# A transformer block's opening in halves: scale weights by column halves, first queries by halves, six heads projected ahead of the shift

## The chip, the cores and the metric

The kernel runs on one core of a Trainium2 chip. Its engines work side by side, each through its own list of instructions in order: TensorE (PE in the profile: matmuls; PEld: the loading of their stationary operand), VectorE (DVE), ScalarE (ACT), GpSimd (POOL) and SyncE (SP), which here issues most of the loads. The metric is the time of one execution on the device in microseconds (us), as the median of the runs; less is better.

## The reference, cut to what matters

One block: a normalisation with scale and shift out of a condition vector, attention over the last keys of a cache, then a gated feed-forward stage.

```python
mod = (_silu(c) @ w_mod).reshape(c.shape[0], 6, 1, -1)
sa, ca, ga, sb, cb, gb = (mod[:, 0], mod[:, 1], ...)
h = _layernorm(x) * (1 + ca) + sa                # x: 2048 tokens x 1024
x = x + ga * _A_ref(h, A_k_cache, A_v_cache, A_wq, A_wo)
h = _layernorm(x) * (1 + cb) + sb
x = x + gb * _B_ref(h, B_w_gate, B_w_up, B_w_down)
# _A_ref: q = h @ wq (32 heads of 128); scores over the last 512 keys (4 key groups);
#         softmax; values; then @ wo.    _B_ref: silu(h @ w_gate) * (h @ w_up) @ w_down
```

All tensors are bf16. `c` is one row of 1024 numbers, `w_mod` 1024 x 6144: its first 1024 columns give the shift `sa`, the next 1024 the scale `ca`, then the gate `ga`.

## The kernel before

Tokens go through in four chunks of 512, each of four tiles of 128. For a chunk, 32 heads are worked one after another in the loop of L1037: queries ahead of time, scores (`scores`, four matmuls of 512 columns into the banks `SCB` 2 to 5), the exponential on ACT (`exps`, two of 1024 numbers a row), the product with the values (`pv`, 16 matmuls of 129 columns), and a reciprocal and a multiplication on DVE. Then comes the output projection, and after the last chunk the feed-forward stage. Queries are projected four heads before they are used (`LEAD`); the first eight heads (`PLAIN`) plainly with 8 matmuls, the others in pairs by seven products that need sums of weights and of inputs (`weight_sums`, `input_sums`, on DVE).

The order of the work is written out by hand. Each `T.op` puts an instruction on one engine's list, with waits on the semaphores of whatever wrote or read its buffers. Nothing reorders it later. DMAs are issued by SP in program order.

The change touches the stretch before the first scores, the opening, and the first heads of the loop. Before the change it goes so:

- SP issues: 4 tiles of x, the scale columns of `w_mod` in 8 row blocks of 256 KB (`load_wm(0)`), the query weights of heads 0 to 3 (`load_wq(0)`, two halves of 512 KB by rows), the keys, the shift columns in 8 row blocks (`load_wm(1)`), the query weights of heads 4 to 7 (`load_wq(1)`), and the values in four parts.
- ACT, DVE and PE turn the condition into 8 columns `sc` (L344 to L350).
- DVE computes mean and variance of tiles 0 and 1 by `ln_stats` and `ln_rstd`; ACT sums up tiles 2 and 3 (`sums_1`), DVE scales these sums (`sums_2`); POOL takes the power -0.5. `ln_norm` writes the normalised tiles.
- PE multiplies the scale columns with `sc` (`mod_open(0, kc)`: 8 matmuls of one column for each row block), with a filler matmul (`keep_warm`) here and there, and turns the tiles (`open_turn`, 8 transposes each), which DVE or ACT evicts into `h_sb[1]`, 128 x 8 x 512. When all eight row blocks are in, DVE forms the gain `g1`, and DVE and ACT multiply the turned input by it, 512 tokens at a time (L514 to L519).
- From L1002: PE projects heads 0, 1 and 2 out of this unshifted input, with the shift columns (`mod_open(1, kc)`) between; DVE copies the shift `sa`; PE turns the keys (`turn_keys`), multiplies the query weights of heads 0 to 3 with `sa`, 32 matmuls of one column, and projects head 3. ACT adds these four columns to the four heads (L1021), and DVE writes the shifted input `h_sb[0]` (L1024), which all later heads read.
- In the loop, iterations 0 to 3 project heads 4 to 7 (`qproj`, 8 matmuls and a copy on DVE). Also in chunk 0, from iteration 0 on, one step of the next chunk's normalisation (`ln1[1]`) is taken in each iteration, and from iteration 3 on steps of the gate's computation (`mod_ga`) (L1074). A step is a load, half of a tile's statistics, a normalisation, or two scaled rows (`ln_scale`, L376).

## Time and profile before

| what | value |
|---|---|
| median of 3 runs | 1174.58 us (1174.24 to 1174.76) |
| the profiled execution | 1188.51 us |
| its span, first to last instruction | 1186.7 us |
| granted TensorE clock in it | 0.995 |
| PE busy in the span | 1150.3 us (97%) |
| DVE busy | 814.2 us (69%) |
| ACT busy | 502.1 us (42%) |
| first one-column matmul of the scale | 7.62 us |
| first query matmul | 16.29 us |
| first exponential | 28.56 us |

Times within the profile count from the span's start. A line of the timeline gives start, length, engine, source line, operation, output and input, the count, and in brackets how long the engine had been idle and what ended that. Matmuls and transposes stand under the lines of the helpers that issue them, L265 and L269, so they are told apart by their shapes: 128x1 is a column of scale or shift, 128x512 a query or score matmul, 128x129 a value product. Some matmul records are missing.

### The profile page before, as it was taken

How to read it: one execution, taken by the hardware profiler on the slowest of the kernel's cores; microseconds unless marked ns; L12 is line 12 of the kernel's file. 1: busy time of each engine (PE TensorE's matmuls, PEld its weight loads, DVE VectorE, ACT ScalarE, POOL GpSimd, SP SyncE). 2: the span in 40 equal slices, each digit the busy share in tenths (PEclk: the TensorE clock that was granted, in tenths of full speed). 3: DMA queues.
4: the chain of work that ended last, by engine and by line, in shares of the span. 5: the costliest groups of instructions: out<-in, count | busy, mean ns of one | idle time of the engine just before them, and what ended most of it. 6: DMA issues, size and time to landing. Idle time of an engine off the chain costs nothing.

```text
span 1186.7 us, 20667 instructions
## 1 busy us (share of the span) xinstructions
PE 1150.3 (97%) x7721; PEld 665.4 (56%) x7838; DVE 814.2 (69%) x1800; ACT 502.1 (42%) x750; POOL 20.6 (2%) x41
## 2 busy tenths in 40 slices
PE   6999999999999999999999999999989999999998
PEld 4677646777557776478764444444433444444443
DVE  4888647987638887358857688887335977776214
ACT  4777503666216664056741344444110344444110
POOL 1000000000000000000000000000000000000000
PEclk9999999999999999999999999999989999999999
DMA  9999796999859987769949666566896332321633
GB/s 302 230 262 233 212 364 215 288 251 224 285 188 281 266 204 226 280 181 273 262 104 367 204 183 207 178 188 175 288 176 140 106 106 73 97 82 63 247 134 133
DMA packets 282852, 245.56 MB, mean 207 GB/s; under 512 B 109952, under 2 KB 245120, under 8 KB 282752
## 3 DMA queue, kind: packets, MB, share of 16 engines
q1 hardware_dynamic: 252304, 179.74, 58.2%
q10 hardware_dynamic: 30448, 64.50, 16.0%
q8 instruction: 62, 1.02, 0.4%
q14 instruction: 38, 0.31, 0.1%
HBM read 189.27 MB, written 30.41 MB: 185 GB/s over the span
## 4 chain that ended last, share of the span: by engine, by line
PE 85%; DMA 6%; DVE 4%; issue 2%; SPq 1%; ACT 1%; POOL 0%; POOLq 0%; DVEq 0%
PE ps L265 85%; DMA arena<-arena 3%; DMA arena<-x_mid 1%; DVE arena L580 1%; DMA arena<-in_w_mod_dram 1%; DMA arena<-wq_sums 1%; SPq L284 1%; DVE arena L376 0%; DVE arena L717 0%; DVE arena L412 0%; DVE arena L646 0%; DVE arena L421 0%; DVE arena L919 0%; DVE arena L847 0%; ACT arena L967 0%
## 5 line engine op out<-in xcount | busy, mean ns | idle before, releaser
L265 PE MATMUL ps<-arena 128*128 128x129 bf16 (+5 forms) x7672 | 1146.5, 309 | 28.4 <-DVE arena L469 3.9
L265 PEld LDWEIGHTS ps<-arena 128*128 128x128 bf16 (+1 forms) x7789 | 661.8, 98 | 512.3 <-issue 22.3
L700 ACT ACTIVATE arena<-ps 128x1024 bf16<-128x1024 f32 x256 | 251.3, 1022 | 39.3 <-PE ps L265 36.3
L580 DVE TENSOR_TENSOR arena<-arena 128x512 f16<-128x512 bf16 (+3 forms) x510 | 222.8, 479 | 26.0 <-DMA wo_sums<-arena 11.0
L640 ACT ACTIVATE arena<-ps 128x256 f32<-128x256 f32 x134 | 51.4, 384 | 167.2 <-PE ps L265 166.8
L1211 DVE TENSOR_TENSOR arena<-ps,arena 128x512 f16<-128x512 f32 x112 | 77.1, 688 | 36.9 <-PE ps L265 36.6
L1204 ACT ACTIVATE arena<-ps 128x512 f32<-128x512 f32 x112 | 66.9, 597 | 73.5 <-PE ps L265 73.5
L717 DVE TENSOR_TENSOR arena<-ps,arena 128x512 bf16<-128x512 f32 x128 | 88.5, 691 | 4.5
L1233 ACT ACTIVATE ps<-ps 128x512 f32<-128x512 f32 x56 | 32.6, 582 | 130.3 <-PE ps L265 130.3
L919 DVE TENSOR_TENSOR arena<-ps,arena 128x512 f32<-128x512 f32 x34 | 23.4, 688 | 87.1 <-PE ps L265 87.0
L646 DVE TENSOR_TENSOR arena<-ps,arena 128x256 bf16<-128x256 f32 x180 | 75.5, 419 | 10.9 <-PE ps L265 6.9
L1223 DVE TENSOR_TENSOR arena<-ps,arena 128x512 bf16<-128x512 f32 x56 | 38.5, 687 | 27.3 <-ACT arena L1218 27.3
L716 DVE RECIPROCAL arena<-ps 128x4 f32<-128x4 f32 x128 | 23.0, 180 | 38.1 <-PE ps L265 37.5
L1218 ACT ACTIVATE arena<-ps 128x512 f16<-128x512 f32 x56 | 33.3, 594 | 31.6 <-PE ps L265 31.6
L922 DVE TENSOR_TENSOR arena<-ps,arena 128x512 bf16<-128x512 f32 x22 | 15.1, 688 | 45.3 <-PE ps L265 45.3
L412 DVE BATCH_NORM_STATS2 arena<-arena 128x6 f32<-128x512 bf16 x56 | 38.3, 686 | 6.3 <-DMA arena<-x_mid 6.1
L950 DVE SCALAR_TENSOR_TENSOR arena<-arena 128x512 f32<-128x512 bf16 x56 | 41.6, 742 | 0.1
L1218 ACT ACTIVATE arena<-arena 128x512 f16<-128x512 f16 x56 | 34.9, 622 | 7.7 <-DVE arena L1211 7.7
L847 DVE TENSOR_TENSOR arena<-arena 128x1024 f16<-128x1024 bf16 (+1 forms) x48 | 29.7, 684 | 5.7 <-DMA arena<-arena 5.7
L363 POOL TENSOR_TENSOR arena<-arena 128x1 f32<-128x1 f32 x30 | 18.1, 602 | 877.9 <-DVE arena L361 874.8
L421 DVE TENSOR_SCALAR arena<-arena 128x1024 bf16<-128x1024 bf16 x28 | 15.1, 540 | 25.9 <-DMA arena<-arena 23.9
L871 ACT ACTIVATE arena<-ps 128x512 f32<-128x512 f32 x12 | 6.8, 596 | 59.2 <-PE ps L265 51.3
(62 smaller groups left out, 230.4 us busy)
## 6 DMA issues: line engine op xcount, KB each, us to landing
arena<-wo_sums ACTq DMA_DIRECT2D x46, 512.0 KB, 9.2
arena<-in_A_wq_dram SPq DMA_DIRECT2D x42, 512.0 KB, 5.1
arena<-wq_sums SPq DMA_DIRECT2D x22, 768.0 KB, 6.3
arena<-in_B_w_gate_dram SPq DMA_DIRECT2D x28, 512.0 KB, 4.2
arena<-in_B_w_up_dram SPq DMA_DIRECT2D x28, 512.0 KB, 5.3
arena<-wd_sums ACTq DMA_DIRECT2D x16, 896.0 KB, 7.3
arena<-in_A_wo_dram SPq DMA_DIRECT2D x24, 512.0 KB, 6.4
arena<-in_B_w_down_dram ACTq DMA_DIRECT2D x12, 896.0 KB, 7.9
```

The costliest lines, as they stand in the source:

```text
L265: T.op(PE, lambda: TE.matmul(out_ap, lhsT, rhs, start=start, stop=stop, skip_group_check=loose), reads=reads, writes=bb)
L412: T.op(DVE, lambda: V.bn_stats(st_sb[i][:, 6 * hf:6 * hf + 6], x_[:, 512 * hf:512 * hf + 512]), reads=[bx], writes=[B_st[i]])
L580: T.op(st, lambda: e.tensor_tensor(dst, x, y, op), reads=reads, writes=[dst_b])
L640: T.op(ACT, lambda: A.activation(sn[k], bank(QBK, 256), AF.Copy), writes=PB[QBK] + [B_sn[k]])
L646: T.op(DVE, lambda: V.tensor_tensor(dst, bank(XBK, 256, off), sn[k], ALU.add), reads=[B_sn[k]], writes=PB[XBK] + [B_q[i % NQ]])
L700: T.op(ACT, lambda: A.activation(ex[i % NEX][:, kt:kt + 2, :], bank(SCB[kt], 1024).rearrange("p (a b) -> p a b", a=2), AF.Exp, scale=att_s ...
L717: T.op(DVE, lambda: V.tensor_tensor(o_sb[i % NOS].rearrange("p (a b) -> p a b", a=TPC), num, rl_bc, ALU.mult), reads=[B_rl], writes=both + ...
L950: T.op(DVE, lambda: V.scalar_tensor_tensor(acc, ms[:, kc, :], sc[:, kc:kc + 1], acc, op0=ALU.mult, op1=ALU.add), reads=[B_ms, B_sc, B_acc] ...
L1204: T.op(ACT, lambda: A.activation(fn[m][i], bank(b), AF.Copy), writes=PB[b] + [B_fn[m][i]])
L1211: T.op(DVE, lambda: V.tensor_tensor(ring[c_], bank(b), fn[m][i], ALU.add), reads=[B_fn[m][i]], writes=PB[b] + [bs[c_]])
L1218: T.op(ACT, lambda: A.activation(sl_[c_], src, AF.Silu), reads=reads, writes=writes + [B_sl[c_]])
L1223: T.op(DVE, lambda: V.tensor_tensor(dst, u_[0], s_[0], ALU.mult), reads=[s_[1]] + [x for x in u_[1:]], writes=[db] + list(bb))
```

## The change

The scale columns are loaded and multiplied in two column halves of four pieces of 256 KB each, with half of the first query weights between. Each half of the gain is formed as soon as its half is done. The input is multiplied by it in pieces of one contraction block and 256 tokens, and heads 0 to 3 are projected in the same pieces: lower contraction blocks for the first 256 tokens, then for the others, then the upper ones. Heads 4 and 5 are projected in the opening as well, from unshifted input, so six heads get a shift column afterwards; two of these additions are on ACT and four on DVE. Both halves of the second query weights are loaded before the shift columns, and the keys are turned before these are multiplied. Thirteen filler matmuls run before the first column of the scale. The mean's negation for tiles 2 and 3 goes from DVE to ACT. In the loop, iterations 0 to 3 project heads 6 and 7 by halves, and the next chunk's normalisation takes its first step in iteration 4.

The diff, with 12 columns of indentation taken off the lines inside the block, blank lines and unchanged lines left out:

```diff
...
-    shift, B_shift = small("shift", 4, F32)
+    shift, B_shift = small("shift", 6, F32)
+    B_shift = [B_shift, _Buf("shift1")]
...
-B_wm = bufs("wm", 2 * DT)
-wm = M.take(AT_OT * KB, [2 * DT, D], BF16, B_wm)
-def load_wm(which):
+B_ca = [bufs("ca%d_" % i, DT // 2) for i in range(2)]
+B_sw = bufs("sw", DT)
+wm = M.take(AT_OT * KB, [2 * DT, D], BF16, B_ca[0] + B_ca[1] + B_sw)
+def load_ca(half):
+    for kp in range(DT // 2):
+        T.op(Q_wm[half * DT // 2 + kp], lambda: SP.dma_start(
+            wm[:, 2 * kp:2 * kp + 2, half * 512:half * 512 + 512],
+            w_mod[kp * 256:(kp + 1) * 256, D + half * 512:D + half * 512 + 512].rearrange("(k p) n -> p k n", p=P)),
+            writes=[B_ca[half][kp]])
+def load_sa():
...
-        T.op(Q_wm[which * DT + kc], lambda: SP.dma_start(
-            wm[:, which * DT + kc, :], w_mod[kc * P:(kc + 1) * P, (1 - which) * D:(2 - which) * D]),
-            writes=[B_wm[which * DT + kc]])
-load_wm(0)
+        T.op(Q_wm[DT + kc], lambda: SP.dma_start(wm[:, DT + kc, :], w_mod[kc * P:(kc + 1) * P, 0:D]), writes=[B_sw[kc]])
+load_ca(0)
...
-def load_wq(gi):
+def load_wq(gi, halves=(0, 1)):
...
-    for j in range(2):
+    for j in halves:
...
-load_wq(0)
+load_wq(0, (0,))
+load_ca(1)
+load_wq(0, (1,))
...
-load_wm(1)
...
+load_sa()
...
+def keep_warm(n):
+    for _ in range(n):
+        mm(bank(SCB[3]), warm[:, 0:P], warm, True, True, [B_warm], PB[SCB[3]])
+keep_warm(8)
...
-def mod_open(which, kc, b):
+GBK, SFT = (QBK, XBK), SCB[1]
+TBK = (OBK, OBK + 1, SCB[1], OBK + 1)
+B_o = [bufs("o%d_" % i, DT) for i in range(2)]
+B_g1h = [_Buf("g1h"), B_g1]
+def scale_column(half, kp):
+    for kc in (2 * kp, 2 * kp + 1):
+        for j in range(DT // 2):
+            mm(bank(GBK[half], 1, j), wm[:, kc, half * 512 + j * P:half * 512 + (j + 1) * P], sc[:, kc:kc + 1],
+               kc == 0 and j == 0, kc == DT - 1, [B_ca[half][kp], B_sc], PB[GBK[half]], loose=True)
+def scale_done(half):
+    lo, hi = 4 * half, 4 * half + 4
+    T.op(DVE, lambda: V.tensor_scalar(g1[:, lo:hi], bank(GBK[half], 4), 1.0, None, op0=ALU.add),
+         writes=PB[GBK[half]] + [B_g1h[half]])
+    T.op(DVE, lambda: V.tensor_copy(g1f[:, lo:hi], g1[:, lo:hi]), reads=[B_g1h[half]], writes=[B_g1f])
+def shift_column(kc):
...
-        mm(bank(b, 1, j), wm[:, which * DT + kc, j * P:(j + 1) * P], sc[:, kc:kc + 1],
-           kc == 0 and j == 0, kc == DT - 1, [B_wm[which * DT + kc], B_sc], PB[b], loose=True)
+        mm(bank(SFT, 1, j), wm[:, DT + kc, j * P:(j + 1) * P], sc[:, kc:kc + 1],
+           kc == 0 and j == 0, kc == DT - 1, [B_sw[kc], B_sc], PB[SFT], loose=True)
...
-    b = SCB[tt]
+    b = TBK[tt]
...
+def open_evict(tt):
+    b = TBK[tt]
...
-    if tt in (1, 2):
-        T.op(ACT, lambda: A.activation(dst, src, AF.Copy), writes=PB[b] + [B_hn[1][tt]], after=B_h[1])
+    if tt == 2:
+        T.op(ACT, lambda: A.activation(dst, src, AF.Copy), writes=PB[b] + [B_hn[1][tt]])
...
-        T.op(DVE, lambda: V.tensor_copy(dst, src), writes=PB[b] + [B_hn[1][tt]], after=B_h[1])
-def keep_warm(n):
-    for _ in range(n):
-        mm(bank(XBK), warm[:, 0:P], warm, True, True, [B_warm], PB[XBK])
+        T.op(DVE, lambda: V.tensor_copy(dst, src), writes=PB[b] + [B_hn[1][tt]])
+def open_scale(th, kc, st=DVE):
+    x_ = h_sb[1][:, kc, 256 * th:256 * th + 256]
+    rd = B_hn[1][2 * th:2 * th + 2]
+    if st is ACT:
+        T.op(ACT, lambda: A.activation(x_, x_, AF.Copy, scale=g1f[:, kc:kc + 1]), reads=rd + [B_g1f], writes=[B_o[th][kc]])
+    else:
+        T.op(DVE, lambda: V.tensor_scalar(x_, x_, g1[:, kc:kc + 1], None, op0=ALU.mult),
+             reads=rd + [B_g1h[kc // 4]], writes=[B_o[th][kc]])
+Q0 = [SCB[0], SCB[2], SCB[3], OBK, OBK + 1, QBK]
+def q_open(i, kcs, th):
+    for kc in kcs:
+        mm(bank(Q0[i], 256, 256 * th), wq_sb[0][:, kc, hd(i) * P:(hd(i) + 1) * P], h_sb[1][:, kc, 256 * th:256 * th + 256],
+           kc == 0 and th == 0, kc == DT - 1, [B_wq[0][kc // 4], B_o[th][kc]], PB[Q0[i]], loose=True)
...
-    T.op(DVE, lambda: V.tensor_scalar(xsum[tt][:, 1:2], xsum[tt][:, 0:1], -1.0 / D, None, op0=ALU.mult),
+    T.op(ACT, lambda: A.activation(xsum[tt][:, 1:2], xsum[tt][:, 0:1], AF.Copy, scale=-1.0 / D),
...
-for tt in range(2):
-    ln_stats(tt, tt, 0)
-    ln_stats(tt, tt, 1)
-    ln_rstd(tt)
-    if tt == 0:
-        sums_1(2)
+keep_warm(5)
+ln_stats(0, 0, 0)
+ln_stats(0, 0, 1)
+ln_rstd(0)
+sums_1(2)
+ln_stats(1, 1, 0)
+ln_norm(0, 0, n0[0], B_n0[0])
+ln_stats(1, 1, 1)
+ln_rstd(1)
...
-ln_norm(0, 0, n0[0], B_n0[0])
...
-ln_norm(1, 1, n0[1], B_n0[1])
-ln_norm(2, 2, n0[2], B_n0[2])
-sums_2(3)
-mod_open(0, 0, QBK)
+scale_column(0, 0)
...
-mod_open(0, 1, QBK)
-keep_warm(1)
-mod_open(0, 2, QBK)
+scale_column(0, 1)
...
-mod_open(0, 3, QBK)
+open_evict(0)
+ln_norm(1, 1, n0[1], B_n0[1])
+scale_column(0, 2)
+keep_warm(1)
+scale_column(0, 3)
+scale_done(0)
+sums_2(3)
+ln_norm(2, 2, n0[2], B_n0[2])
+keep_warm(4)
...
-mod_open(0, 4, QBK)
+open_evict(1)
+for kc in range(4):
+    open_scale(0, kc, ACT if kc == 3 else DVE)
...
-mod_open(0, 5, QBK)
+open_evict(2)
+ln_norm(3, 3, n0[3], B_n0[3])
...
-mod_open(0, 6, QBK)
-mod_open(0, 7, QBK)
-ln_norm(3, 3, n0[3], B_n0[3])
-T.op(DVE, lambda: V.tensor_scalar(g1, bank(QBK, DT), 1.0, None, op0=ALU.add), writes=PB[QBK] + [B_g1])
-T.op(DVE, lambda: V.tensor_copy(g1f, g1), reads=[B_g1], writes=[B_g1f])
+q_open(0, range(4), 0)
+q_open(1, range(4), 0)
...
-keep_warm(1)
-for kc in (0, 1, 2, 3, 6, 7):
-    T.op(DVE, lambda: V.tensor_scalar(h_sb[1][:, kc, :], h_sb[1][:, kc, :], g1[:, kc:kc + 1], None, op0=ALU.mult),
-         reads=B_hn[1] + [B_g1], writes=[B_h[1][kc]])
-for kc in (4, 5):
-    T.op(ACT, lambda: A.activation(h_sb[1][:, kc, :], h_sb[1][:, kc, :], AF.Copy, scale=g1f[:, kc:kc + 1]),
-         reads=B_hn[1] + [B_g1f], writes=[B_h[1][kc]])
+open_evict(3)
+q_open(2, range(4), 0)
+scale_column(1, 0)
+scale_column(1, 1)
+q_open(3, range(4), 0)
+for kc in range(4):
+    open_scale(1, kc, ACT if kc == 3 else DVE)
+scale_column(1, 2)
+scale_column(1, 3)
+scale_done(1)
+for i in range(4):
+    q_open(i, range(4), 1)
+for th in range(2):
+    for kc in range(4, 8):
+        open_scale(th, kc, ACT if kc > 5 else DVE)
+for th in range(2):
+    for i in range(4):
+        q_open(i, range(4, 8), th)
...
-        b = SCB[1 + i // 8]
+        b = (QBK, XBK)[i // 8]
...
-                                        bank_bf(SCB[1 + j])[:, 0:8 * P].rearrange("p (a b) -> p a b", a=8)),
-             writes=PB[SCB[1 + j]] + [B_kT[j]])
-def q_plain(i, b, slot):
+                                        bank_bf((QBK, XBK)[j])[:, 0:8 * P].rearrange("p (a b) -> p a b", a=8)),
+             writes=PB[(QBK, XBK)[j]] + [B_kT[j]])
+def qproj(i, b, half):
...
-    for kc in range(DT):
-        mm(bank(b), wq_sb[sl][:, kc, hh * P:(hh + 1) * P], h_sb[slot][:, kc, :], kc == 0, kc == DT - 1,
-           [B_wq[sl][kc // 4], B_h[slot][kc]], PB[b])
-def qproj(i, b):
-    q_plain(i, b, 0)
-    T.op(DVE, lambda: V.tensor_copy(q_sb[i % NQ], bank(b)), writes=PB[b] + [B_q[i % NQ]])
+    for kc in range(4 * half, 4 * half + 4):
+        mm(bank(b), wq_sb[sl][:, kc, hh * P:(hh + 1) * P], h_sb[0][:, kc, :], kc == 0, kc == DT - 1,
+           [B_wq[sl][kc // 4], B_h[0][kc]], PB[b])
+    if half:
+        T.op(DVE, lambda: V.tensor_copy(q_sb[i % NQ], bank(b)), writes=PB[b] + [B_q[i % NQ]])
...
-SFT = SCB[0]
-Q0 = [OBK, OBK + 1, QBK, XBK]
-q_plain(0, Q0[0], 1)
-q_plain(1, Q0[1], 1)
-for kc in range(3):
-    mod_open(1, kc, SFT)
-q_plain(2, Q0[2], 1)
-for kc in range(3, DT):
-    mod_open(1, kc, SFT)
+NOP = len(Q0)
+def q_more(i, kcs):
+    for kc in kcs:
+        mm(bank(Q0[i]), wq_sb[1][:, kc, (hd(i) % 4) * P:(hd(i) % 4 + 1) * P], h_sb[1][:, kc, :], kc == 0, kc == DT - 1,
+           [B_wq[1][kc // 4], B_o[0][kc], B_o[1][kc]], PB[Q0[i]])
+def q_shifted(i, st):
+    dst, c_ = q_sb[i % NQ], shift[:, i:i + 1]
+    if st is ACT:
+        T.op(ACT, lambda: A.activation(dst, bank(Q0[i]), AF.Identity, bias=c_), reads=[B_shift[i > 0]], writes=PB[Q0[i]] + [B_q[i % NQ]])
+    else:
+        T.op(DVE, lambda: V.tensor_scalar(dst, bank(Q0[i]), c_, None, op0=ALU.add), reads=[B_shift[i > 0]], writes=PB[Q0[i]] + [B_q[i % NQ]])
+def shifted_input(kc):
+    T.op(DVE, lambda: V.tensor_scalar(h_sb[0][:, kc, :], h_sb[1][:, kc, :], sa[:, kc:kc + 1], None, op0=ALU.add),
+         reads=[B_o[0][kc], B_o[1][kc], B_sa], writes=[B_h[0][kc]])
+turn_keys()
+q_more(4, range(DT))
+for kc in range(4):
+    shift_column(kc)
+q_more(5, range(2))
+for kc in range(4, DT):
+    shift_column(kc)
...
-turn_keys()
-for i in range(4):
-    for kc in range(DT):
-        mm(bank(SFT, 1, DT + i), wq_sb[0][:, kc, hd(i) * P:(hd(i) + 1) * P], sa[:, kc:kc + 1], i == 0 and kc == 0,
-           kc == DT - 1, [B_wq[0][kc // 4], B_sa], PB[SFT], loose=True)
-T.op(DVE, lambda: V.tensor_copy(shift, bank(SFT, 4, DT)), writes=PB[SFT] + [B_shift])
-for i in range(4):
-    if i == 3:
-        q_plain(3, Q0[3], 1)
-    T.op(ACT, lambda: A.activation(q_sb[i], bank(Q0[i]), AF.Identity, bias=shift[:, i:i + 1]),
-         reads=[B_shift], writes=PB[Q0[i]] + [B_q[i]])
-for kc in range(DT):
-    T.op(DVE, lambda: V.tensor_scalar(h_sb[0][:, kc, :], h_sb[1][:, kc, :], sa[:, kc:kc + 1], None, op0=ALU.add),
-         reads=[B_h[1][kc], B_sa], writes=[B_h[0][kc]])
+shifted_input(0)
+q_more(5, range(2, 4))
+def shifts(heads, b):
+    for n, i in enumerate(heads):
+        for kc in range(DT):
+            mm(bank(b, 1, DT + n), wq_sb[i // 4][:, kc, (hd(i) % 4) * P:(hd(i) % 4 + 1) * P], sa[:, kc:kc + 1],
+               n == 0 and kc == 0, kc == DT - 1, [B_wq[i // 4][kc // 4], B_sa], PB[b], loose=True)
+    lo, hi = heads[0], heads[-1] + 1
+    T.op(DVE, lambda: V.tensor_copy(shift[:, lo:hi], bank(b, hi - lo, DT)), writes=PB[b] + [B_shift[lo]])
+shifts([0], XBK)
+for kc in range(1, 5):
+    shifted_input(kc)
+shifts(list(range(1, NOP)), SFT)
+q_more(5, range(4, DT))
+q_shifted(0, ACT)
+q_shifted(1, DVE)
+q_shifted(2, ACT)
+for kc in range(5, DT):
+    shifted_input(kc)
+q_shifted(3, DVE)
+q_shifted(4, DVE)
+q_shifted(5, DVE)
...
+for kc in range(DT):
+    B_h[1][kc].absorb(B_o[0][kc])
+    B_h[1][kc].absorb(B_o[1][kc])
...
-        qproj(i + LEAD, (QBK, XBK)[i % 2])
+        qproj(NOP + i // 2, (XBK, QBK)[i // 2], i % 2)
...
-        for g_ in ([ln1[1]] if 1 in ln1 else []) + [mod_ga] * (i > 2) * (1 if i < 8 else i % 2 if i < 20 else 1 + i % 2):
+        for g_ in [ln1[1]] * (i > 3) + [mod_ga] * (i > 2) * (1 if i < 8 else i % 2 if i < 20 else 1 + i % 2):
...
-      24: lambda: T.op(ACT, lambda: A.activation(shift, shift, AF.Silu), reads=[B_shift], writes=[B_shift]),
+      24: lambda: T.op(ACT, lambda: A.activation(shift, shift, AF.Silu), reads=B_shift, writes=B_shift),
```

## The prediction

> **What bounds the kernel now.** I read the page first, then the chain of waits over the first 80 us, then the timeline of the same stretch and the landing times of its loads. The page:
>
> ```profile
> PE 1150.3 (97%) x7721; PEld 665.4 (56%) x7838; DVE 814.2 (69%) x1800; ACT 502.1 (42%) x750; POOL 20.6 (2%) x41
> PE 85%; DMA 6%; DVE 4%; issue 2%; SPq 1%; ACT 1%; POOL 0%; POOLq 0%; DVEq 0%
> ```
>
> TensorE (PE) sets the end. The change only reorders work of the first chunk's start, so the question is how much earlier PE gets through it. The chain of waits there, with start and length:
>
> ```profile
> 13.83 9.80 DMA arena<-in_w_mod_dram
> 23.63 0.05 issue
> 23.67 0.35 PE ps L265 x8
> 24.02 0.92 PE ps L269 x16
> 24.94 0.78 PE ps L265 x32
> ```
>
> Until 23.63 us the chain is the load queue: the last row block of the shift weights is issued at 13.83 and lands 9.80 later. After it come its 8 one-column matmuls, the key transposes, and the 32 shift matmuls. The timeline of all engines:
>
> ```profile
> 16.29 7.05 PE L265 MATMUL ps<-arena 128*128 128x512 bf16 x79 [1.05 <-DVE arena L515]
> 23.67 0.35 PE L265 MATMUL ps<-arena 128*128 128x1 bf16 x8 [0.33 <-DMA arena<-in_w_mod_dram]
> 24.78 5.58 PE L265 MATMUL ps<-arena 128*128 128x1 bf16 x52
> ...
> 34.28 1.94 ACT L700 ACTIVATE arena<-ps 128x1024 bf16<-128x1024 f32 x2 [1.73 <-PE ps L265]
> 37.78 1.94 ACT L700 ACTIVATE arena<-ps 128x1024 bf16<-128x1024 f32 x2 [1.56 <-PE ps L265]
> 41.28 1.94 ACT L700 ACTIVATE arena<-ps 128x1024 bf16<-128x1024 f32 x2 [1.56 <-PE ps L265]
> ```
>
> The first query matmul starts at 16.29. From the head loop on, exps come every 3.50 us and ACT waits for PE 1.56 of it: PE is the bound of the first heads. Matmul spacing, from the timeline of PE in short stretches (start, time to the last end, count):
>
> ```profile
> 16.99 2.98 PE L265 MATMUL ps<-arena 128*128 128x512 bf16 x13
> ```
> ```profile
> 24.86 0.79 PE L265 MATMUL ps<-arena 128*128 128x1 bf16 x26
> ```
>
> A 512-column matmul lasts 0.38 but starts every (2.98 - 0.38)/12 = 0.216 us; a one-column one every (0.79 - 0.16)/25 = 0.025; the warm transposes after 23.89 every 0.056 in the same way. Check: one early head is 8 + 4 matmuls of 0.216 and 16 of 0.057 (129 columns): 1.73 + 0.86 + 0.91 = 3.50, the exp period. I take 256 columns at half of 0.216, 0.108.
>
> The query weights' loads (the tile's own view):
>
> ```profile
> L301 SPq DMA_DIRECT2D arena<-in_A_wq_dram x8: 374/413/661, 6.7 to 40.9; - x8
> DMA to landing us min/median/max: 3.3/6.6/11.7
> ```
>
> The longest, 11.7, is the second half of group 1 (issued at 14.78): it lands at 26.5.
>
> [...] The landings agree: they follow issue order, so what is issued ahead of the shift weights delays them. [...] here 512 KB in 1 KB pieces take 1.5 us (the two halves of query group 0: 6.69 + 7.1 and 7.26 + 8.0) against 0.68 per 256 KB in 2 KB rows.
>
> **The change part by part, against the profiled execution's own time** (span 1186.7, whole 1188.5; the median shown is 1174.6; I carry a difference in us over unchanged).
>
> *Load order.* Before the last shift-weight block there were x 1 MB, scale 2, query group 0 1, keys 0.5, shift 2. Group 1 (1 MB) now goes ahead too. So the block lands where group 1 ended, 26.5, plus 8 scale pieces of 256 KB that now have 1 KB rows: 8 x (0.75 - 0.68) = 0.55. I take 27.1, which is 3.4 later than 23.63. Bounds: 26.5 (1 KB rows cost nothing) to 28.4 (one more delay like that of 1.3 us on the landings at 17.5 to 19.5). Values, behind all of these in both kernels, land at about 28.8 and are first used at 33.
>
> *The opening up to that landing.* The 8 early fillers run cold, 0.43 each (twice 0.216), from 1.2 to 4.7, so the transpose of the condition moves from 3.59 to 4.7 and VectorE's (DVE's) first statistics from 3.88 to 5.0. Against this DVE loses a 1.72 us wait for ACT at 7.45 (the mean's negation is now on ACT). Following the issue orders with the row durations (evictions 0.69, normalisations 0.54, statistics 0.69, ACT's copy 1.02): scale half 0 has landed at about 10, half 0 of the gain is ready at 11.3, the first two token tiles are turned and evicted at 12.8, and half-width scales follow. Those are not in the trace: 512 columns start every 0.28, so 256 lie between 0.14 and 0.28 on DVE and up to 0.71 on ACT; I take 0.15 and 0.4. First query matmul at 13.0, 3.3 earlier than 16.29. Then PE has 64 x 0.108 = 6.9 for four heads, 32 scale matmuls 0.8, tile 3's transposes 0.45: done about 21.3. Key transposes 0.9 to 22.2, head 4 8 x 0.216 to 23.9, four shift columns and two matmuls of head 5 to 25. PE then waits for the loads, about 1.5 us before 27.1. That slack hides the fillers, the DVE delay, and what the half-width operations cost over my values; if the cover went, each us of them would show.
>
> *After the landing.* Before: 23.67 to the first scores at 27.5, 3.85 (transposes, 32 shift matmuls, head 3's 1.73). After: shift column 0.2, two matmuls of head 5 0.43, shift of head 0 0.2 (with a 0.1 wait for its DVE copy), 40 more shift matmuls 1.0, head 5's last four 0.86: first scores at 29.9, 2.4 later than before, with two heads (16 x 0.216 = 3.45) more done. DVE now adds the shift to heads 1, 3, 4, 5 (0.69 each), where ACT did it to four; head 1's, due for its scores, is done at 30.4, and its bank for the third score at that time: 0.2 of wait.
>
> *Head loop, heads 0 to 3.* Each does 4 query matmuls instead of 8. In the first, scores(1) now reaches banks that the exps (2 x 1.02) have not freed: 0.45 idle. So the first value product starts at 33.1, against 31.0. Then 0.86 + 0.86 + 0.91 = 2.63 per head instead of 3.50, ACT's 2.04 still under it: the fourth starts at 33.1 + 7.9 = 41.0, against 41.5. DVE from the shift copy to the fourth normalisation has some 15 us of work in that time (6 evictions of 0.69, 4 of 0.83, 8 shifted inputs 0.28, 6 sums of 0.68 and small ones), ends at about 43.3, and the fifth value product, which needs it, is due at 44.0: just covered. Head 7's copy now empties the bank that the next product needs, about 0.1 late. Net -0.4. Query group 2's load waits for the last shift matmul and is issued at 29.2 instead of 26.7, lands by 36, and is used by DVE at 38.5: hidden. Loads for the next chunk's normalisation leave SP's queue here.
>
> *The next chunk's normalisation* moves from heads 0-21 to heads 4-25, one step a head: 3 loads, 8 statistics, 4 normalisations, 4 turned tiles on SP, 8 scales. It leaves heads 4 to 6, where DVE was 95% busy, and its four scale steps (0.64 each) move to heads 22 to 25, where the gate task takes 1.5 steps of 0.74 a head. Two heads there take:
>
> ```profile
> 101.70:108.30 6.60, 5.97 (x14) 1.00 0.92 206
> 108.30:115.00 6.70, 5.99 (x13) 1.00 0.94 302
> ```
>
> (window, its length, DVE busy). 6.0 with two more scale steps, 1.28, less the one already in the first, is over 6.6 by up to 0.7, twice: 0 to +1.4 for PE. But in heads 20 and 21, where both fell together, PE waited 0.5 and 0.7 (at 97.1 and 106.1), which goes. Gain at heads 4 to 6 at most 0.6. Bounds -0.6 to +1.4; I take +0.2.
>
> Sum: +3.4 (landing), -1.05 (3.85 to 2.8 after it), +0.2 (bank), -0.4 (first head: 0.86 less, 0.45 idle), -2.6 (three heads at 0.87), +0.1 (copy): about -0.4. With +0.2 of the normalisation, -0.2 us. 1174.6 - 0.2 = 1174.4.
>
> **Rivals.**
> PE is the bound throughout, because the shift weights land early. For: 3.3 earlier start, less 0.8 + 0.45 + 0.4 (16 more shift matmuls) of new work, plus about 1.0 of idle before 27.5 that goes, less 0.45: 2.2 saved, with the 0.6 of heads 4 to 6 2.8: 1171.8. Against: the block would have to land by about 25.3, and 1 MB more at this rate does not.
> DVE becomes the bound, in heads 0 to 8 or 22 to 25: +1.4 instead of +0.2, 1175.6, no change by the measure below. For: DVE is 94% busy from 45 to 65 us. Against: 69% over the kernel; the backlog is worked off after head 26.
> The array goes cold in the wait before 27.1, and the time ends slower. Price: the cold stretch at the start lasted 7.15 us; at half rate that costs up to 3.6, so about +3.4: 1177.8. [...] Against: at 14.9 to 16.3 PE idled 1.05 and at 22.1 to 23.9 had one-column matmuls alone, and it stayed at full rate.
>
> **How the numbers follow.** A measurement of this kernel tells 0.2%, 2.35 us, from no change. As worked 0.60 (1172.9 to 1176.0); DVE bound 0.12; early loads 0.12; cold array or another late wait 0.16. So faster 0.12, same 0.72, slower 0.16. The range reaches from near the early case to near the cold one: 1172.0 to 1177.3; the likeliest case's own is 1172.9 to 1176.0.
>
> **What would show it.** Last shift-weight landing at 26.5 to 27.6 on the chain; first 512- or 256-column query matmul near 13; transposes at 0.056 from the first; first exp near 30.5; exps 2.6 apart over heads 1 to 3; fourth value product within 1 us of 41; new DVE-ended waits of PE between 102 and 116. Wrong if the landing is outside 26 to 28.5, PE does not reach it waiting, or the steps after it are cold.

## The result and the profile after

In the first comparison the changed kernel took 1178.66 us (median of four runs, 1176.86 to 1180.64), the kernel before 1174.44 (1174.24 to 1174.76): a ratio of 1.0036 [1.0019, 1.0053], 4.2 us slower. The forecast was 1174.4. Two later comparisons on other occasions, with 20 and 14 runs of the same changed kernel, gave 1.0007 [0.9990, 1.0023] and 1.0008 [0.9989, 1.0028]: no difference that can be told. (Below, one run of 1732 us at a clock of 0.66 is left out, and of the four runs of the cut kernel after, those of 212.61 and 212.90 us had a lower clock than the other two.) So two questions stand: did the opening do what was worked out, and where did the first 4.2 us come from.

The page of the kernel after (its profiled execution took 1179.14 us, the span is 1177.2), busy times first, then the shares of the chain that ended last:

```profile
PE 1151.7 (98%) x7784; PEld 669.0 (57%) x7902; DVE 817.2 (69%) x1808; ACT 502.0 (43%) x753; POOL 20.2 (2%) x41
PE 86%; DMA 6%; DVE 4%; issue 2%; SPq 2%; ACT 1%; POOL 0%; POOLq 0%; DVEq 0%
```

Nothing of the balance has changed: TensorE sets the end as before. Its chain of waits over the opening (start, length):

```profile
17.67 9.92 DMA arena<-in_w_mod_dram
27.59 0.05 issue
27.64 0.35 PE ps L266 x8
27.99 0.08 issue
28.07 1.60 PE ps L266 x49
...
30.34 0.76 DVE arena L1077
...
31.14 6.02 PE ps L266 x50
```

The last block of the shift weights lands at 27.59 (23.63 before), and what follows it is short: eight one-column matmuls, the shift matmuls, one eviction with the shift added (line 1077). From the timeline (start, length, operation), PE before and in that wait, and the first exps:

```profile
15.53 7.08 PE L266 MATMUL ps<-arena 128*128 128x256 bf16 x88
22.44 1.06 PE L270 MATMUL ps<-arena 128*128 128x128 bf16 x16
23.55 3.72 PE L266 MATMUL ps<-arena 128*128 128x512 bf16 x65
27.64 3.35 PE L266 MATMUL ps<-arena 128*128 128x1 bf16 x62 [0.37 <-DMA arena<-in_w_mod_dram]
...
35.86 1.94 ACT L763 ACTIVATE arena<-ps 128x1024 bf16<-128x1024 f32 x2 [0.84 <-PE ps L266]
38.49 1.94 ACT L763 ACTIVATE arena<-ps 128x1024 bf16<-128x1024 f32 x2 [0.69 <-PE ps L266]
41.13 1.94 ACT L763 ACTIVATE arena<-ps 128x1024 bf16<-128x1024 f32 x2 [0.70 <-PE ps L266]
```

The queries of four heads are done before the key transposes at 22.44, the last one-column matmuls wait for the load, and the exps of heads 2, 3 and 4 are 2.63 and 2.64 apart (3.50 before). Head 4 starts its exp at 41.13; before it was 41.28.

**Where the two profiles part.** I take the starts of the exps as marks, since both kernels have the same 256 of them. Heads 0 to 31 are the first chunk, 32 to 63 the second, 127 is the last. All in us; the last column is from the last exp to the end, which holds the output projection's end and the whole feed-forward part.

| kernel, run | last shift weights land | head 0 | head 4 | heads 4 to 28 | heads 48 to 64 | after the last exp |
|---|---|---|---|---|---|---|
| before | 23.6 | 28.56 | 41.28 | 81.02 | 55.88 | 576.3 |
| before, a copy | 23.3 | 28.27 | 40.98 | 81.04 | 55.47 | 563.2 |
| after | 27.6 | 31.02 | 41.13 | 81.09 | 53.99 | 568.9 |
| after, second run | 26.3 | 31.49 | 41.96 | 81.35 | 53.98 | 567.7 |
| after, third run | 27.1 | 32.23 | 42.62 | 81.02 | 53.98 | 570.9 |

Three things are to be seen. The stretch that the prediction worked through (up to head 28) moved by 0.1 us in the first pair. In the second chunk, which the prediction took as unchanged, the kernel after is 1.5 to 1.9 us faster. And the last column varies by 13 us, more than anything else, and does so in both kernels: the copy of the kernel before, which is the same code, ends 13.1 us sooner after its last exp. The first profile of after starts its last head's exp at 607.5 us, the copy of before at 609.4: so in this execution the opening and the four chunks were 1.9 us ahead, and all that it lost to the copy was lost behind them.

The last column's difference sits in one place, the start of the first down projection. Windows of the kernel after (stretch, length, then busy time of PE, PEld, DVE, ACT, POOL, then PE's clock, DMA share, GB/s), and DVE's waits in it (us in total, times, longest):

```profile
825.00:880.00 55.00, 54.23 (x250) 24.44 (x251) 21.53 (x48) 8.86 (x15) 2.75 (x5) 1.00 0.87 240
880.00:935.00 55.00, 50.79 (x231) 22.29 (x233) 43.13 (x91) 7.57 (x13) 1.65 (x3) 1.00 0.53 152
```
```profile
DVE arena L436 <- DMA arena<-arena: 16.6, 3, 10.3
```

PE is idle for 5.0 us there, and before that DVE waits 16.6 us for three transposes on the SP queue, one of them 10.3. (Line 436 writes a normalised tile into a buffer out of which a transpose still has to read an earlier one.) The same place in the kernel before's profile, with PE's own waits for a load as a third view:

```profile
880.00:935.00 55.00, 49.54 (x206) 21.10 (x210) 34.74 (x71) 4.08 (x8) 1.65 (x3) 0.91 0.63 147
```
```profile
DVE arena L421 <- DMA arena<-arena: 23.9, 4, 12.5
```
```profile
PE ps L265 <- DMA arena<-wd_sums: 3.5, 2, 3.3
```

There the transposes were later still (23.9 us of waits), PE idled 6.2 us between 825 and 935, and from its two longest gaps on (3.3 and 2.4 us) the clock was at half for 10.2 us in all. More than half of the idling ended with a load of weight sums on ACT's queue, so it isn't the transposes alone that came late. The copy of before shows none of this:

```profile
825.00:880.00 55.00, 55.00 (x256) 24.93 (x255) 26.99 (x61) 9.85 (x17) 3.29 (x6) 1.00 0.85 261
880.00:935.00 55.00, 55.00 (x257) 24.80 (x255) 42.30 (x88) 9.63 (x17) 1.10 (x2) 1.00 0.46 137
```
```profile
DVE arena L421 <- DMA arena<-arena: 5.1, 2, 2.6
```

No line of this stage is in the diff. Over all thirteen profiles of whole kernels, those of the experiments below included, the two things go together: in four DVE waits 15.2 to 23.9 us for these transposes and PE idles 3.9 to 7.6 us between 825 and 935; in the other nine DVE waits 3.8 to 6.6 us and PE idles 0 to 0.7.

### The profile page after: what moved, and what is told of

It reads as the page before. It is cut to its first block, busy times and chain, and to the rows that moved or that the text cites. A ratio compares the mean times of both kernels' runs of the same rounds, so it can differ in the third digit from the quotient of the medians.

```text
span 1177.2 us, 20801 instructions
## 1 busy us (share of the span) xinstructions
PE 1151.7 (98%) x7784; PEld 669.0 (57%) x7902; DVE 817.2 (69%) x1808; ACT 502.0 (43%) x753; POOL 20.2 (2%) x41
## 4 chain that ended last, share of the span: by engine, by line
PE 86%; DMA 6%; DVE 4%; issue 2%; SPq 2%; ACT 1%; POOL 0%; POOLq 0%; DVEq 0%
PE ps L266 86%; DMA arena<-arena 3%; DMA arena<-x_mid 1%; DMA arena<-in_w_mod_dram 1%; DVE arena L643 1%; DVE arena L985 1%; DVE arena L780 0%; DVE arena L982 0%; SPq L287 0%; SPq L294 0%; SPq L309 0%; DVE arena L427 0%; DVE arena L986 0%; DVE arena L391 0%; DVE arena L709 0%
## 5 line engine op out<-in xcount | busy, mean ns | idle before, releaser
L266 PEld LDWEIGHTS ps<-arena 128*128 128x128 bf16 (+1 forms) x7853 | 665.4, 98 | 501.9 <-issue 13.1
L1314 DVE TENSOR_TENSOR arena<-ps,arena 128x512 bf16<-128x512 f32 x56 | 38.5, 688 | 27.1 <-ACT arena L1309 27.1
L985 DVE TENSOR_TENSOR arena<-ps,arena 128x512 bf16<-128x512 f32 x22 | 15.2, 689 | 45.7 <-PE ps L266 45.7
L436 DVE TENSOR_SCALAR arena<-arena 128x1024 bf16<-128x1024 bf16 x28 | 15.2, 543 | 19.2 <-DMA arena<-arena 16.6
```

What stands on the lines that cost most here:

```text
L266: T.op(PE, lambda: TE.matmul(out_ap, lhsT, rhs, start=start, stop=stop, skip_group_check=loose), reads=reads, writes=bb)
L1314: T.op(DVE, lambda: V.tensor_tensor(dst, u_[0], s_[0], ALU.mult), reads=[s_[1]] + [x for x in u_[1:]], writes=[db] + list(bb))
```

## The experiments

**Both kernels again, and the normalisation alone.** Four kernels on one chip: the two unchanged, and the two with only the start of the next chunk's normalisation exchanged.

```diff
# after, with the normalisation from head 0
-for g_ in [ln1[1]] * (i > 3) + [mod_ga] * ...
+for g_ in ([ln1[1]] if 1 in ln1 else []) + [mod_ga] * ...
# before, with the normalisation from head 4: the reverse
```

> The kernel before once more, for a second profile: the first one was 1188.5 us where its runs take 1174.5, so stages cannot be compared with it as they stand. Theory 1 (the opening costs nothing, the loss is made later): exponential number 32 of this profile again near 136.4 us, within 0.3 of the changed kernel's 136.4, and the stages after head 127 some 4 us shorter than the changed kernel's 568.9. Theory 2 (the opening itself costs 4 us, and the first profile of before hid it): head 32 near 132.4, the rest alike. Time 1174.5 either way.

> The changed kernel once more, on the same chip as the others: 1177 to 1180 us if the loss is its own. Theory 1: the waits of the matmuls that differ from before lie after 600 us, and their sum differs from profile to profile. Theory 2: the waits are the same in each profile, and before 140 us.

> The changed kernel with the next chunk's normalisation starting at head 0 again. Rival (DVE is the bound in heads 22 to 25, where scale steps and gate steps meet): 1 to 2 us faster than the changed kernel, head 32 earlier by as much. Theory 1: head 32 within 0.5 us of the changed kernel's, and the time moves, if at all, by what happens after 600 us.

> The kernel before with this one part of the change: the normalisation of the next chunk starts at head 4. Rival (DVE): 1 to 2 us slower than before. Theory 1: head 32 within 0.5 us of before's; if the time of the later stages depends on how their loads happen to meet, even this may move the total by some us while head 32 stays.

Measured against 63 runs of the kernel before (median 1175.38, 1172.97 to 1179.21): the copy of before 1175.40, ratio 1.0005 [0.9991, 1.0019]; after 1175.52, 1.0007 [0.9990, 1.0023]; after with the normalisation from head 0 1176.21, 1.0009 [0.9994, 1.0023]; before with it from head 4 1176.05, 1.0000 [0.9985, 1.0015]. The 4.2 us did not come back. The copies' own runs spread over 11 us (1171.72 to 1182.85) and those of after over 15. Moving the normalisation back did not help: heads 4 to 28 then take 81.6 instead of 81.0 to 81.4, since the 1.0 gained in heads 24 to 28 is more than lost in heads 4 to 8 (13.19 instead of 12.36), 8 to 12 and 20 to 24. The profiles showed the scatter's place, and that a half clock appears in the wait of the opening (26.2 to 33.0 in the second run of after).

**The first chunk alone.** To measure the opening without what comes later, both kernels were cut after the first chunk's attention and output projection. Left out is everything else: three chunks and the feed-forward part; the first chunk's rows are written to all four quarters of the output. One more has eight 512-column fillers around the last four columns of shift matmuls (the edit is shown below; the expectations, written before, count ten), one is without the fillers before the first transposes (`keep_warm(8)` and `keep_warm(5)` removed).

> The kernel before, cut after the first chunk's output projection; the four tiles are then written to all rows of the output. Left out: chunks 1 to 3 and the feed-forward stage. Its own time, some 220 to 240 us, is the base for the next three; without the later stages it should scatter by less than 1 us where the whole kernel scatters by 10.

> The changed kernel cut in the same way (the same left out). Theory 1 (the opening costs next to nothing): -0.4 to +1.2 us against the cut kernel before: the upper end where the array falls to half clock in the wait for the shift weights, as two of three profiles show it. Theory 2 (the 4 us of the first comparison are the opening's): +4.

> The cut changed kernel with two filler matmuls of 512 columns before and between the last four shift columns, so that the array doesn't idle while it waits for their loads (ten fillers, 2.2 us if none fits into the wait). Cold-array theory: no half-clock window after 25 us, 0.5 to 1.2 us faster than the cut changed kernel. Rival (the load alone sets it): the same within 0.3, or slower by up to 0.4 for the fillers that end after a landing.

> The cut changed kernel without the eight fillers ahead of the condition's transpose. As predicted, what they do lies under the wait for the shift weights: within 0.3 us of the cut changed kernel. If the early warm-up matters: slower by 1 or more, with the first query matmuls at half rate and no wait at the last shift column.

Four runs each: before 210.64 (209.53 to 211.68), after 211.87 (209.24 to 212.90), with fillers in the wait 210.82 (210.06 to 211.65), without the early fillers 211.39 (210.77 to 212.75). The ranges overlap, and each scatters by 1.6 to 3.7 us where less than 1 was expected, so alone this shows no more than that the opening and the first chunk cost less than 4 us. The middle, +1.2, and the fillers' -1.05 hang on two runs of after, 212.61 and 212.90 (the others are 209.24 and 211.12); they were taken into the next step as things to test, no more. The half clock came behind the landing in the cut kernel after (29.3 to 32.7) and not in the one with fillers. Without the early fillers the array turned to full rate at 13.8 instead of 4.5 to 6.8 and the first 256-column matmul started at 14.63, yet head 4's exp came at 41.14, as in the first profile of after: in this one profile the early fillers were not needed.

**The first down projection mended.** In that stage the task that normalises the next 1,024 rows starts behind four loads of residual rows on the SP queue. The edit, the same in both kernels, creates it first and lets it issue its three row loads ahead of them:

```diff
 if n == 1:
-    for k in range(4):
-        xr[4 + k] = load_rows(Q_xr[k], t0 + 4 + k, 6 + 2 * k, True)
     if st + 1 < NST:
         tasks.append(ln_task(...))
+        for _ in range(3):
+            next(tasks[-1])
+    for k in range(4):
+        xr[4 + k] = load_rows(Q_xr[k], t0 + 4 + k, 6 + 2 * k, True)
```

The fourth kernel of this group also has the fillers in the opening's wait:

```diff
 q_more(5, range(2))
+fill(2)
 for kc in range(4, DT):
     shift_column(kc)
+    fill(2 * (kc < DT - 1))
```

> The kernel after, unchanged, against the kernel before on the same chip. Theory 1 (the first comparison's 4 us come from the scatter of one stage that both kernels share, the start of the first down projection; the opening itself costs 0 to 2.3 us): mean 0 to 2 us over before, interval includes 1.0010, spread of 5 us or more. Theory 2 (the change itself costs 4 us, by a stall that it makes likelier there): again +3 to +5 us, ratio 1.003 to 1.004.

> The kernel before with one edit in the first down projection: the three row loads of the next normalisation are issued ahead of the four residual loads. Theory 1: the first transposes then have landed before the down projection's matmuls need what follows them; the stall of PE between 825 and 935 us is under 1 us in the profile, the tail from the last exp of the first chunk to the end is 563 us (it was 563 to 576), the runs lie within 4 us of each other, the median is 2 to 4 us under before. Rival: the transposes are late because of the weight loads on ACT's queue, whatever order SP has; then the stall and the scatter stay and the time is within 1 us of before.

> The kernel after with the same edit in the first down projection. Theory 1: it has the same tail as the kernel before with that edit, and differs from it by the opening and the first chunk alone, 0 to +2.3 us (middle +1). Theory 2: +3 us or more against it, since the change would cost time in another place than that stage.

> The kernel after with the same edit and with ten 512-column fillers placed around the last four columns of the shift matmuls, where PE waits for the last shift weights. Theory 1: no half clock between 26 and 34 us, which is worth 0 to 1 us against the kernel without the fillers (the first-chunk pair showed 1.05 with overlapping runs), so it comes out level with the kernel before with the edit, within 1 us. Rival (the cold array costs nothing, since other waits take it up): within 0.3 us of the kernel without fillers.

| kernel | runs | median, range | ratio to before [interval] |
|---|---|---|---|
| before, in this group | 51 | 1175.36, 1172.27 to 1179.01 | |
| after, third run | 14 | 1175.31, 1172.08 to 1183.30 | 1.0008 [0.9989, 1.0028] |
| before, mended | 13 | 1174.88, 1173.84 to 1180.53 | 1.0002 [0.9988, 1.0015] |
| after, mended | 14 | 1174.85, 1172.82 to 1177.01 | 0.9997 [0.9987, 1.0007] |
| after, mended, fillers | 22 | 1173.38, 1172.18 to 1177.50 | 0.9982 [0.9974, 0.9991] |

In the mended kernel before, the same windows and the same line of DVE's waits read:

```profile
825.00:880.00 55.00, 55.00 (x256) 24.95 (x255) 32.84 (x77) 8.85 (x15) 4.39 (x8) 1.00 0.92 271
880.00:935.00 55.00, 55.00 (x257) 24.85 (x255) 36.73 (x70) 10.01 (x18) 0.00 (x0) 1.00 0.35 121
```
```profile
DVE arena L421 <- DMA arena<-arena: 6.4, 2, 3.5
```

PE never stops, and the wait for the transposes is 6.4 us instead of 23.9. By itself this proves nothing, since the unmended copy looked the same (5.1). None of four mended profiles has the stall, four of nine unmended ones do. From the last exp to the end the mended before takes 562.8, the mended after 565.4 and the one with fillers 562.3, against 563 to 576 of the others. (The mended after, at 565.4, still lost 0.7 there and 1.5 more than the mended before between 610 and 825.) In time the rival was near the truth: the medians fell by 0.5 us, within the noise, not by 2 to 4, and the runs of the mended before spread over 6.7 us, not 4. What goes is the upper tail. Of 61 runs of mended kernels (with the one below) one is over 1179.3; of 122 runs of whole kernels without the mend, the unchanged kernel before left out, 24 are. (No expectation names this mark; at 1179.0 it is 2 against 28.) So the rival that weight loads on ACT's queue make the transposes late whatever SP's order is falls as to the stall, though not as to the median. Of the 164 runs of the kernel before that stood beside the others, though, only one is (1184.41), against three of the 20 of its copy. Why the copy scatters more than the original is open, and it warns against reading 1 us out of a comparison with the original; the new kernels are better compared with each other.

With that stage mended, before and after have the same median (1174.88 and 1174.85; by the means after is 1.0 ahead). Theory 2, that the change costs 3 us or more in some other place, falls. Whether it makes the late stall likelier is not settled: 17 of 70 runs with the new opening are over 1179.3 and 7 of 52 with the old one, or 8 of 216 if the original's runs are counted in.

What sets the stall off is open. The third transpose of the task took 13.1 to 16.7 us from issue to landing in the four stalled profiles and 3.4 to 6.7 in the five other unmended ones. In all nine a pair of weight-sum loads was issued on ACT's queue right behind it, 0.4 to 1.3 us in the stalled ones and 1.1 to 2.0 in the others, and in the kernel before these loads were slow as well (15.2 and 18.3 us, in its copy 6.8 and 9.1). Slow transposes and slow weight sums came together; whether one slows the other is not shown, since no run set that distance on purpose.

The fillers show what the half clock costs. The wait in the opening of the mended after, without and with fillers (the column before the last two is PE's clock):

```profile
22.00:26.00 4.00, 3.77 (x68) 2.41 (x65) 0.96 (x2) 0.00 (x0) 0.00 (x0) 1.00 1.13 338
26.00:30.00 4.00, 3.51 (x62) 2.18 (x63) 2.70 (x10) 1.37 (x2) 0.00 (x0) 0.65 0.24 48
30.00:34.00 4.00, 4.00 (x11) 1.39 (x10) 2.71 (x6) 1.94 (x2) 0.00 (x0) 0.50 0.98 313
```
```profile
26.00:30.00 4.00, 4.00 (x87) 2.65 (x84) 1.73 (x7) 0.69 (x1) 0.00 (x0) 1.00 0.24 53
30.00:34.00 4.00, 3.84 (x25) 1.71 (x24) 3.68 (x8) 3.53 (x4) 0.00 (x0) 1.00 0.85 276
```

Without fillers the array runs at half clock from 27.2 to 34.0 and issues 11 matmuls between 30 and 34; with them it stays at full clock and issues 25. The exp of head 4 starts at 42.32 and 41.15, although the last shift weights land at 26.44 without fillers and only at 27.29 with them; counted from the landing it is 15.88 and 13.85, 2.0 apart. The medians differ by 1.5 (the means, 1174.87 and 1173.85, by 1.0, with 0.2 to 1.8 as a resampled 95% interval). The rival that a cold array costs nothing here falls. After with both edits is the fastest of all, and the only one whose interval excludes no change; the comparison is with the original, under the warning above.

**Why the second chunk is faster.** The gain of 1.5 to 1.9 us between heads 48 and 64 is nearly all one exp period, heads 57 to 58: 4.9 to 5.2 us in the kernel before and its copy, 3.52 in all profiles of after. The timeline of before's copy shows why:

```profile
276.04 0.69 DVE L580 TENSOR_TENSOR arena<-arena 128x1024 f16<-128x1024 bf16 x1 [1.87 <-DMA arena<-wq_sums]
...
276.79 0.61 PE L265 MATMUL ps<-arena 128*128 128x256 f16 x4 [0.44 <-DVE arena L580]
```

DVE has waited 1.87 us for a load of stored weight sums, and everything of that head queues behind it. The second run of after has the same instruction without any wait:

```profile
274.72 0.68 DVE L643 TENSOR_TENSOR arena<-arena 128x1024 f16<-128x1024 bf16 x1
```

From 10 us ahead of head 48's exp to 14 us behind it DVE's instructions start at the same times in both, to 0.01 us. SP's queue, however, gets through its transposes and loads sooner in after, and issues that load 18.8 instead of 21.4 us behind head 48's exp. Two parts of the change could set that: the 1024 extra packets of the halved loads, or the order of the opening. Each was taken alone.

```diff
# before, scale weights in halves (with and without the mended stage)
-load_wm(0)                       # 8 loads of 128 rows x 1024 columns
+for kp in range(DT // 2):        # 8 loads of 256 rows x 512 columns
+    for hf in range(2):
+        ... wm[:, 2*kp:2*kp+2, hf*512:hf*512+512] ...
# after, scale weights in rows
-load_ca(0); load_wq(0, (0,)); load_ca(1); load_wq(0, (1,))
+load_ca(0); load_ca(1); load_wq(0, (0,)); load_wq(0, (1,))   # 4 loads of 128 rows x 1024 columns each
```

> The kernel before, with one part of the change alone: the scale weights arrive in eight loads of two row blocks by half the columns (1 KB pieces, 1024 more packets on SP's queue) instead of eight loads of one row block (2 KB). Order and count of the loads stay. Theory A (the 1.4 to 1.6 us that the kernel after gains in the second chunk, where heads 57 to 58 take 3.52 instead of 4.9 to 5.2, come with the extra packets, which shift where SP's queue stalls): 3.52 between these two heads, the first exp up to 0.6 late, 0 to 1 us faster than before. Theory B (they come with the order of the opening, which this kernel does not change): 4.9 to 5.2, and 0 to 0.6 us slower.

> The kernel after with the scale weights loaded as before, in eight row blocks of 2 KB pieces, all ahead of the first query weights. Theory A: heads 57 to 58 take 4.9 to 5.2, and the gain of the second chunk is gone: 1.4 us slower than the kernel after. Theory B: 3.52, and the chunk stays at 54.0 between heads 48 and 64. On either, the last shift weights land up to 0.6 us earlier than the 26.3 to 27.6 of the kernel after, and the first 256-column query matmul starts 1 to 3 us later than 13.6.

> The kernel before with the scale weights in halves and the three row loads moved ahead in the first down projection. Theory A: both gains add, 1.4 us under the kernel before with the moved loads alone (median 1175.0), about 1173.5, level with the kernel after with moved loads and fillers (1173.4). Theory B: 1175.0 to 1175.6.

Heads 57 to 58 took 4.26 in before with halves, 4.85 in the mended one with halves, and 3.52 in after with rows. So the gain stays without the extra packets, and they alone don't bring it, though 4.26 lies between the two theories and they may carry a part: theory A falls, the order of the opening is what goes with the gain (3.52 or 3.53 in all seven profiles of a whole kernel with the new order, 4.26 to 5.2 in all six with the old one). Which of the moved instructions shifts SP's queue 200 us later stays open. The times against 39 runs of before (1175.39): before with halves 1175.78, 1.0011 [0.9997, 1.0026]; mended with halves 1175.53, 1.0001 [0.9992, 1.0010]; after with rows 1176.23, 1.0009 [0.9989, 1.0029]. In the last the array was at half clock from 8.6 to 15.4, the first 256-column matmul started at 16.48 instead of 12.4 to 14.1, and PE was late for the landing (26.8, no earlier than in after): the first exp came at 32.88. That fits the purpose of the halves, to let the first queries start early, but the half clock lies ahead of them too, and this one profile can't part the two. What the halves cost as a load is within the scatter: in the kernels with the old opening the last shift weights land at 23.26 and 24.07 with halves and at 22.75 to 23.63 without.

## Why the prediction was right and wrong

**Right: what bounds it, the landing, and the order of events.** SP's first 25 loads landed in the order of their issue in both first profiles (in before those issued at 6.69, 7.26, 7.84, 8.73, 13.83, 14.30 and 14.78 at 13.8, 15.3, 16.7, 17.4, 23.6, 25.1 and 26.5; in after the last, issued at 17.67, at 27.6). The landing was to be 27.1; it was 26.3 to 27.6 in six profiles of whole kernels with the new loads. PE was to reach it waiting: without fillers it did, for 0.5 to 0.9 us in several pieces and not 1.5 in one. First exp "near 30.5": 31.0 to 32.2. "Exps 2.6 apart over heads 1 to 3": 2.63, once 2.78. The first query matmul was forecast at 13.0 and started between 12.4 and 13.1 in five of the six, at 14.1 in the first.

**Right as long as the array stays warm: the sum over the stretch that was worked out.** The scatter of the landing drops out when head 4's exp is counted from it:

| opening | from the landing to head 4's exp, us |
|---|---|
| old, six of seven profiles | 17.65 |
| old, normalisation from head 4; the array cold until 20.2 | 19.10 |
| new, full clock there: after; with fillers; cut, with fillers; cut, no early fillers | 13.53; 13.85; 13.92; 13.81 |
| new, at half clock for 3.4 us: normalisation from head 0; cut | 14.74; 15.33 |
| new, at half clock for 6.8 us: second run; third run; mended | 15.65; 15.56; 15.88 |
| new, scale in rows; PE late for the landing | 16.16 |

The forecast's terms behind the landing add up to -3.75; warm, they measured -3.7 to -4.1. The landing itself came 3.7 later on the average (26.9 against 23.2 in four profiles without halves), for +3.4 forecast. So up to head 4 the warm opening is level or a few tenths ahead (-0.15 in the first pair), for -0.4 forecast. Heads 4 to 28, with the moved normalisation, take 0.0 to +0.5 more in five runs of after (with and without edits elsewhere) and +1.3 in the one with the scale in rows, for +0.2. In the first pair these add up to -0.1, against -0.2. So neither the rival of an early landing nor that of DVE as the bound was right: DVE does lose 1.0 in heads 24 to 28, but gains 0.6 in heads 4 to 12 and 0.6 in 20 to 24. One reading was off without bearing on the sum: PE's waits at 97.1 and 106.1 were 0.34 and 0.52 us and not 0.5 and 0.7. A cold array shows in the spacing of matmuls (512 columns 0.43 us apart in after from 1.59 to 4.15, against 0.216), less in their length (three fillers of before at 7.5 to 9.7 took 587 ns each, 13 such matmuls from 16.99 on 380).

**Not settled: the term "+0.55" for shorter pieces.** Halves land 0.5 later in the kernel before (mean of two against four profiles) and 0.1 later in the new opening (six against one), within the 1 us by which the landing itself varies from execution to execution.

**Wrong: that the array stays warm in the wait.** The prediction gave the cold array 0.16 (with "another late wait") and argued that one-column matmuls alone had kept the clock up at 22.1 to 23.9; what brings it down, the first 80 us of before do not show, so the chance was an estimate. In four of the five profiles of a whole kernel with the new opening's loads and no fillers there (the three runs of after, the one with the normalisation from head 0, the mended one) the clock fell to half for 3.4 or 6.8 us, from 26.2 to 29.2 on; only the first had it elsewhere (10.2 to 13.6). So the chance was far too low. The price, "+3.4", came from the cold stretch at the start of before (7.62 to 14.77; its transposes were 0.107 us apart, those from 23.89 on 0.056), and was too high: by the table 1 to 2 us by head 4, and 1.0 to 1.5 in the whole. Both errors together are about +1 us: the five start head 4 at 41.1 to 42.6, mean 41.9, and six profiles of kernels with the old opening at 40.4 to 42.1, mean 41.2, so the opening costs +0.7 where -0.4 was forecast. With fillers it is 41.15.

**Not seen: the second chunk.** The prediction ended its account with the first chunk. -1.5 to -1.9 us came from a wait for weight sums that went with the old opening, 200 us later. It covers the cold array's cost: the last head's exp starts at 608.8 on the average of seven profiles with the new opening and at 609.2 of six with the old one.

**The step that failed** is "the change only reorders work of the first chunk's start, so the question is how much earlier PE gets through it", together with the measure, "0.2%, 2.35 us". Both took what follows as a constant. The chain after the first chunk isn't one: what follows the last exp differed by 13.1 us between two executions of the same code, most of it at the start of the first down projection (6.2 us of idle PE and 10.2 us at half clock in one, neither in the other), and three runs within 0.5 us had hidden it. The first comparison's 4.2 us is not reproduced by 34 later runs of the same kernel, and none of it can be found in the stretch that was forecast (-0.1). In the profiled one of its four runs the stall explains it: 5.0 us of idle PE in a stage that the copy of before passes with none. That the other three drew it too is argued and not shown, since they left no profile, and it would be bad luck: of the 34 later runs 12 reached the lowest of the four, so four in four has an estimated chance of about 1 in 60. Something peculiar to that first occasion isn't excluded; why its median was 4.2 us up stays open.

A range that held this would have had to add that scatter, seen or bounded from the trace: DVE's 23.9 us of waits for transposes, with PE's windows at 49.54 of 55, stood in the profile of before.

## What to carry to other kernels

Before a change of 1 us is priced, find the largest wait of the whole trace that ends with a transfer while two queues are loading (here DVE's 23.9 us for transposes): it may be far from the change, and decides what a measurement can tell. When an opening is shortened down to a load, look at the clock in the wait that is left; with matmuls of one column in it the clock fell to half in five of eight profiles here, and eight 512-column ones put into that gap were worth 1.0 to 1.5 us. Mark both traces by an instruction that they share and compare interval by interval to the end; the gain of the second chunk was found only so.

## What the runs showed of the hardware

In the opening the clock fell to half without a long idle: in the mended after PE's only gaps over 0.15 us between 20 and 30 us were 0.23 and 0.49, with one-column matmuls around them, and the half clock began 0.7 us after the second. It came in stretches of 3.41 and 6.83 us. The length of the gaps alone doesn't decide it here. The cut after fell to half at 29.3 with no gap over 0.15 us between 20 and 32, behind one-column matmuls without a pause; and the copy of before had three gaps of 0.28 to 0.38 us among its one-column matmuls between 21 and 24 and stayed at full rate. In the first down projection the clock of before fell to half in a gap of 3.3 us and at the end of one of 2.4, while the third run of after waited 2.5 us for a load there and stayed at 1.00. What the runs show is that it varies from execution to execution: of the eight profiles with the new opening and no fillers there, five fell to half between 26.2 and 29.3, in or behind a stretch of one-column matmuls, and three did not; of two with fillers neither did. What tips it is open.

In the first down projection DVE waited 15.2 to 23.9 us for the SP queue's transposes in four profiles, while weight sums came in on ACT's queue. The same loads stood beside the transposes in the profiles without a stall (3.8 to 6.6 us). How far the two queues held each other up was not measured.
